# Sliding-window attention and a gated MLP in one kernel: scores of two chunks back to back, and another order for the prologue

## The chip, the cores and the metric

The kernel runs on one core of a Trainium2 chip. The metric is the device time of one execution in microseconds, given as the median of nine executions. The profile comes from one further execution of the same kernel.

## The reference

Attention over q, k and v of the shape 8 batches x 8 heads x 576 positions x 64, where a query sees itself and the 63 positions before it, and then a gated MLP over the 4608 tokens of width 512, with d_ff = 1536:

```python
scores = scale * np.matmul(q, k.transpose(0, 1, 3, 2))        # scale = 1/8
mask = (rel >= 0) & (rel < 64)                                # rel = query position - key position
attn = softmax(where(mask, scores, -1e9));  x = (attn @ v)    # heads laid side by side: 4608 x 512
g = x @ w_gate
out = (g / (1 + exp(-g)) * (x @ w_val)) @ w_out               # 4608 x 512, float32
```

## The kernel before

The 4608 tokens are cut into 36 chunks of 128 tokens for the attention and into 9 blocks of 512 tokens for the MLP; four chunks make a block. TensorE (PE) does all the multiplying, in bf16:

- `S(n)`: the scores of chunk n, sixteen small matmuls (64 rows x 64 columns), into two PSUM banks. ScalarE takes the exponential of each bank into the tile `pt`, and VectorE multiplies it with the 0/1 mask. With `bias` the mask is put in beforehand by two matmuls with `nmask`, and VectorE's two products fall away.
- `AV(n)`: sixteen matmuls of `pt` with the values, two banks; VectorE divides by the sums (`rc`) and writes `xb`.
- `X(n)`: the transpose of `xb` into `xT`, as a DMA transpose on SyncE's queue ("sp"), or on PE with a copy by ScalarE or VectorE.
- `T(n, x)` / `Tpe(n, x, engine)`: the transpose of a loaded k or q chunk into `kT` or `qT`, by a DMA on SP or on PE with a copy.
- `shift(n, part)`: a copy of half a value chunk into `vb` (by DMA on SP, ScalarE or VectorE).
- `F(c, f0, nf, u0, u1)`: for block c, `nf` slices of 128 hidden units by the chunks u0 to u1: matmuls with Wg, ScalarE's tanh into `sig`, matmuls with Wv, and two VectorE operations into `hT`. A block has 12 slices; a full slice is eight matmuls of 128x512.
- `O(c, u)`: twelve matmuls of `hT` with Wo for one chunk of outputs, ScalarE's copy into `ost`, a DMA to memory.

Loads are DMAs issued by GpSimd (POOL), in one queue: `ld` loads a k, q or v chunk (two DMAs where the chunk crosses a batch), `W` some slices of Wg or Wv, `load_wo` half of Wo. A `ld` with a third number also waits until that chunk's scores have run on PE. k and q have rings of four buffers, so a load into a buffer waits until the chunk before it there has been transposed.

Each engine works through its own instructions in the order in which the program lists them, and waits on semaphores. Up to the first instructions of block 2, the order is written out in `PLAN`, a list made beforehand: it starts with clearing tiles (`init_va`, `init_pt` and others), warm-up matmuls on PE (`warm`), the loads, and goes through blocks 0 and 1 of `F`, the outputs of block 0, and the scores up to chunk 12. From block 2 on a loop repeats one period for each chunk.

PSUM has eight banks: four ("f", 0 to 3) for F in turn, one ("o", bank 4) for O, and three ("a", 5 to 7) in turn for scores, AV and transposes. During PLAN, before the first O, bank 4 is in the turn of "a".

Of the kernel before, what the change touches and what calls it, by code (L numbers as in the profile page):

```python
# [5 lines left out]
ALU = mybir.AluOpType  # L6

B, H, S, D = 8, 8, 576, 64
DM, DFF = H * D, 1536
T = B * S  # L10
NCH = T // 128
NFC = T // 512
# [136 lines left out]

class _Kernel:  # L150
    PLAN = [
        ('first_loads', 0), ('init',), ('init_va', 8, 9), ('ld', 'v', 2), ('first_loads', 1), ('init_va', 0, 1),
        ('init_mask',), ('first_cast', 0, 'q', 'act'), ('warm', 4), ('first_cast', 1, 'k', 'act'), ('warm', 5),
        ('ld', 'k', 2), ('init_va', 1, 2), ('first_cast', 1, 'q', 'act'), ('init_va', 6, 7),
        ('first_cast', 0, 'k', 'dve'), ('Tpe', 0, 'k', 'dve'), ('ld', 'q', 2), ('Tpe', 0, 'q', 'dve'), ('warm', 4),
        ('init_pt', 2, 'dve'), ('ld', 'k', 3), ('init_va', 3, 4), ('warm', 2), ('init_kT',), ('init_pt', 1, 'dve'),
        ('shift', 0, 0, 'dve'), ('Tpe', 1, 'k', 'dve'), ('init_va', 2, 3), ('ld', 'v', 1), ('init_pt', 0, 'act'),
        ('ld', 'q', 3), ('shift', 2, 0, 'dve'), ('init_vb',), ('ld', 'k', 4), ('Tpe', 1, 'q', 'act'),
        ('shift', 0, 1, 'act'), ('S', 0, True), ('ld', 'q', 4), ('ld', 'v', 3), ('S', 1, True), ('init_va', 9, 10),
        ('shift', 2, 1, 'dve'), ('ld', 'k', 5), ('Tpe', 2, 'k', 'dve'), ('Tpe', 2, 'q', 'dve'), ('ld', 'q', 5),  # L160
        ('W', 'g', 0, 2), ('init_pt', 3, 'dve'), ('warm', 2), ('Tpe', 3, 'k', 'dve'), ('W', 'v', 0, 2),
        ('ld', 'v', 4), ('shift', 1, 0, 'act'), ('AV', 0), ('S', 2, True), ('init_va', 4, 5), ('init_va', 5, 6),
        ('W', 'g', 2, 4), ('Tpe', 3, 'q', 'dve'), ('shift', 1, 1, 'act'), ('W', 'v', 2, 4), ('AV', 1),
        ('Tpe', 4, 'k', 'dve'), ('W', 'g', 4, 7), ('X', 0, 'act'), ('shift', 3, 0, 'act'), ('Tpe', 4, 'q', 'dve'),
        ('S', 3, True), ('AV', 2), ('S', 4, True), ('W', 'v', 4, 7), ('AV', 3), ('ld', 'q', 7), ('X', 2, 'dve'),
        ('X', 1, 'act'), ('Tpe', 5, 'q', 'dve'), ('ld', 'v', 5), ('Tpe', 5, 'k', 'act'), ('X', 3, 'dve'),
        ('shift', 3, 1, 'act'), ('F', 0, 0, 2, 0, 2), ('W', 'g', 7, 10), ('shift', 4, 0, 'act'), ('ld', 'q', 6),
        ('F', 0, 0, 2, 2, 4), ('AV', 4), ('F', 0, 2, 1, 0, 4), ('S', 5), ('F', 0, 3, 1, 0, 4), ('ld', 'k', 7),
        ('X', 4, 'dve'), ('F', 0, 5, 2, 0, 2), ('F', 0, 4, 3, 3, 4), ('shift', 5, 0, 'act'), ('shift', 5, 1, 'act'),
        ('F', 1, 0, 4, 0, 1), ('W', 'v', 7, 10), ('shift', 4, 1, 'act'), ('Tpe', 7, 'q', 'act'), ('ld', 'k', 6),  # L170
        ('F', 0, 4, 1, 0, 2), ('AV', 5), ('ld', 'k', 9), ('F', 1, 4, 2, 0, 1), ('Tpe', 7, 'k', 'act'),
        ('ld', 'v', 6), ('W', 'g', 10, 12), ('ld', 'q', 9), ('init_va', 7, 8), ('ld', 'k', 8), ('F', 0, 7, 1, 0, 4),
        ('X', 5, 'act'), ('Tpe', 6, 'k', 'dve'), ('Tpe', 6, 'q', 'act'), ('ld', 'k', 10), ('shift', 6, 0, 'act'),
        ('F', 0, 8, 1, 0, 4), ('S', 7), ('F', 1, 0, 4, 1, 2), ('F', 0, 4, 3, 2, 3), ('S', 6), ('ld', 'v', 7),
        ('ld', 'q', 10), ('Tpe', 8, 'k', 'act'), ('F', 0, 9, 1, 0, 4), ('F', 1, 4, 4, 1, 2), ('shift', 6, 1, 'act'),
        ('W', 'v', 10, 12), ('T', 10, 'q'), ('T', 9, 'q'), ('shift', 7, 0, 'act'), ('Tpe', 10, 'k', 'act'),
        ('ld', 'v', 8), ('AV', 6), ('ld', 'q', 8), ('Tpe', 9, 'k', 'act'), ('load_wo', 6, 12), ('F', 0, 10, 1, 0, 4),
        ('load_wo', 0, 6), ('ld', 'k', 11), ('AV', 7), ('X', 6, 'act'), ('F', 0, 11, 1, 0, 4), ('ld', 'q', 11),
        ('ld', 'v', 9), ('Tpe', 8, 'q', 'dve'), ('ld', 'v', 13, 7), ('ld', 'v', 10), ('F', 1, 1, 3, 2, 3),
        ('ld', 'q', 13, 7), ('ld', 'v', 11), ('F', 1, 6, 3, 0, 1), ('shift', 8, 0, 'act'), ('X', 7, 'sp'), ('S', 8),  # L180
        ('S', 10), ('ld', 'v', 12, 6), ('F', 1, 9, 2, 0, 2), ('T', 11, 'q'), ('shift', 7, 1, 'act'), ('S', 9),
        ('O', 0, 0), ('shift', 13, 1, 'sp'), ('F', 1, 0, 1, 2, 4), ('shift', 9, 1, 'act'), ('AV', 8),
        ('ld', 'k', 12, 6), ('ld', 'q', 12, 8), ('shift', 10, 0, 'dve'), ('F', 1, 8, 1, 2, 4),
        ('shift', 11, 1, 'dve'), ('Tpe', 11, 'k', 'act'), ('ld', 'k', 13, 8), ('O', 0, 1), ('ld', 'v', 14, 10),
        ('AV', 10), ('shift', 12, 0, 'sp'), ('shift', 11, 0, 'act'), ('F', 1, 8, 1, 1, 2), ('F', 1, 1, 3, 3, 4),
        ('shift', 9, 0, 'act'), ('T', 12, 'k'), ('shift', 8, 1, 'dve'), ('shift', 10, 1, 'act'), ('S', 11),
        ('O', 0, 2), ('AV', 9), ('T', 12, 'q'), ('X', 8, 'sp'), ('F', 1, 11, 1, 0, 4), ('X', 10, 'sp'), ('AV', 11),
        ('X', 9, 'sp'), ('ld', 'q', 16, 10), ('O', 0, 3), ('T', 13, 'k'), ('F', 1, 4, 4, 2, 3), ('S', 12),
        ('ld', 'k', 14, 10), ('X', 11, 'sp'), ('ld', 'q', 15, 11), ('ld', 'q', 14, 8), ('ld', 'k', 16, 10),
        ('shift', 13, 0, 'sp'), ('shift', 14, 0, 'sp'), ('T', 13, 'q'), ('shift', 12, 1, 'sp'), ('ld', 'v', 16, 10),  # L190
        ('ld', 'k', 15, 11), ('shift', 14, 1, 'sp'), ('ld', 'v', 15, 11), ('ld', 'q', 17, 12), ('ld', 'v', 17, 11),
        ('T', 14, 'k'), ('F', 1, 4, 4, 3, 4), ('T', 14, 'q'), ('F', 1, 9, 2, 2, 4), ('ld', 'k', 17, 12),
    ]

    NQ = 4
# [66 lines left out]
    def segs(self, t0, size):  # L262
        r = 0
        while r < size:
            b, s = divmod(t0 + r, S)
            L = min(size - r, S - s)
            yield r, b, s, L
            r += L
# [123 lines left out]
        b1 = (2 * n + 1) % BPB == 0  # L392
        return slice(2, 4) if b0 else (slice(1, 3) if b1 else slice(0, 2))

    def S(self, n, bias=False):
        if n >= NCH:
            return
        g = self.g
        ip, iz = n % self.NP, n % self.NZ
        pt = self.pt[ip]  # L400
        bx = [self.bank("a"), self.bank("a")]
        sv = [b[0][:, :].rearrange("p (w c q) -> p w c q", w=2, c=4) for b in bx]
        nm = self.nmask[:, :].rearrange("p (a q) -> p a q", a=4)[:, self.var(n)]
        nm = nm.unsqueeze(2).to_broadcast([128, 2, 4, 64])
# [18 lines left out]
        m = self.mask[:, :].rearrange("p (a q) -> p a q", a=4)[:, self.var(n)]  # L423
        m = m.unsqueeze(2).to_broadcast([128, 2, 4, 64])
# [174 lines left out]
    def step(self, op, *a):  # L599
# [16 lines left out]
        else:  # L616
            getattr(self, op)(*a)

    def build(self):
        self.phase = 0  # L620
        self.banks("a", [0, 1, 2, 3, 5, 6, 7])
        for s in self.PLAN:
            self.step(*s)
        for c in range(2, NFC):
            for u in range(4):
                n = 4 * c + u + 4
                self.F(c, 3 * u)
                self.AV(n)
                self.T(n + 3, "k")
                self.X(n)  # L630
                self.T(n + 3, "q")
                self.shift_v(n + 3)
                self.F(c, 3 * u + 1)
                self.S(n + 1)
                self.load(n + 6, after=n + 1)
                late = c == NFC - 1 and u == 3
                if not late:
                    self.O(c - 1, u)
                self.F(c, 3 * u + 2)
                if late:  # L640
                    self.O(c - 1, u)
        self.banks("o", [0, 1, 2, 3])
        for u in range(3):
            self.O(NFC - 1, u)
        self.O_last(NFC - 1, 3)
        self.g.emit()
# [42 lines left out]
```

## Time and profile before

| | us |
|---|---|
| median of nine executions (lowest, highest) | 343.31 (342.4, 348.0) |
| the profiled execution, its time | 344.18 |
| the profiled execution, span from first to last instruction | 342.4 |
| first F on PE | 19.66 |
| first instruction of the loop, F(2, 0), on PE | 88.96 |
| end of the loop, start of the last four outputs, on PE | 329.0 |

The span is counted from the first instruction; times below that have no other unit are us from there. The page's rows give each engine's busy time, then the span in 40 slices with busy tenths, then the DMA queues, the chain of waits that ended last, and groups of instructions with their mean duration. The timeline and the answers by stretch come from the same execution's trace.

### The profile page before, as it was taken

The page shows a single profiled execution, that of the slowest core. Times are in us where ns is not written, and L with a number is a line of the kernel's source. Part 1 is how long each engine was busy: PE and PEld are TensorE (multiplying, and loading weights), DVE is VectorE, ACT ScalarE, POOL GpSimd, SP SyncE. Part 2 cuts the span into 40 slices and gives each one's busy share as a digit, 9 for nine tenths or more (in the row PEclk, how much of TensorE's full clock was granted, in tenths as well). Part 3 has the DMA queues.
Part 4 walks back from the last instruction along what each step waited for, and adds up shares of the span by engine and source line. Part 5 has one row for each costly group of instructions (what it writes and reads, how often), then busy time and mean ns, then how long its engine had stood idle before and what let it go on. Part 6 is the DMA issues. An engine that isn't in the chain of part 4 may idle for free.

```text
span 342.4 us, 7138 instructions
## 1 busy us (share of the span) xinstructions
PE 331.4 (97%) x2879; PEld 177.4 (52%) x2879; DVE 218.2 (64%) x475; ACT 147.8 (43%) x257; POOL 106.9 (31%) x133
## 2 busy tenths in 40 slices
PE   7999998899899999999999999999999999999996
PEld 3568776467444444444444444444444444444444
DVE  5868889276766666666666666666666666655520
ACT  4866777364233444433333444444444443223221
POOL 8994480808053334333333334333300000000000
PEclk9999999899999999999999999999999999999999
DMA  9999999999999999999999999999984411100012
GB/s 161 157 194 183 138 151 163 137 206 127 170 149 220 142 139 146 139 142 137 147 121 161 120 161 144 119 139 142 139 139 103 73 46 48 46 31 34 31 61 95
DMA packets 172001, 43.65 MB, mean 128 GB/s; under 512 B 157568, under 2 KB 167488, under 8 KB 171968
## 3 DMA queue, kind: packets, MB, share of 16 engines
q0 software_dynamic: 115200, 18.36, 77.5%
q1 hardware_dynamic: 49504, 15.00, 29.0%
q10 hardware_dynamic: 7264, 9.83, 8.6%
q8 instruction: 23, 0.38, 0.5%
q14 instruction: 10, 0.08, 0.1%
HBM read 37.75 MB, written 9.44 MB: 138 GB/s over the span
## 4 chain that ended last, share of the span: by engine, by line
PE 90%; POOL 4%; DMA 2%; ACT 2%; DVE 1%; issue 0%; POOLq 0%
PE ps L525 53%; PE ps L564 28%; PE ps L415 3%; PE ps L446 2%; PE ps L445 2%; DMA Wv<-in_moe_w_val_dram 2%; POOL kn L340 1%; POOL qn L340 1%; POOL va L340 1%; ACT pt L428 1%; PE ps L586 1%; ACT sig L541 1%; PE ps L498 1%; ACT vb L272 0%; DVE uu L546 0%; DVE hT L548 0%
## 5 line engine op out<-in xcount | busy, mean ns | idle before, releaser
L546 DVE SCALAR_TENSOR_TENSOR uu<-sig,ps 128x512 bf16<-128x512 bf16 (+3 forms) x112 | 74.4, 665 | 96.4 <-ACT sig L541 95.6
L525 PE MATMUL ps<-xT,Wg 128*128 128x512 bf16 (+2 forms) x572 | 111.9, 327 | 1.6 <-DVE hT L548 1.4
L525 PE MATMUL ps<-xT,Wv 128*128 128x512 bf16 (+2 forms) x572 | 111.9, 327 | 0.3 <-DMA Wv<-in_moe_w_val_dram 0.3
L541 ACT ACTIVATE sig<-ps 128x512 bf16<-128x512 f32 (+3 forms) x112 | 65.1, 582 | 97.7 <-PE ps L525 97.7
L564 PE MATMUL ps<-Wo,hT 128*128 128x512 bf16 x420 | 97.8, 384 | 1.4 <-ACT pt L428 1.4
L548 DVE SCALAR_TENSOR_TENSOR hT<-uu,ps 128x512 bf16<-128x512 bf16 (+3 forms) x112 | 74.8, 668 | 4.0
L525 PEld LDWEIGHTS ps<-xT,Wv 128*128 128x128 bf16 x572 | 50.0, 98 | 44.6 <-issue 0.6
L525 PEld LDWEIGHTS ps<-xT,Wg 128*128 128x128 bf16 x572 | 47.7, 98 | 39.1 <-DVE hT L548 1.6
L340 POOL DMA_DIRECT2D kn<-in_k_dram x38 | 33.1, 882 | 106.0 <-PE ps L415 96.5
L564 PEld LDWEIGHTS ps<-Wo,hT 128*128 128x128 bf16 x420 | 39.4, 99 | 47.1 <-issue 2.2
L569 ACT ACTIVATE ost<-ps 128x512 f32<-128x512 f32 x35 | 20.9, 597 | 67.7 <-PE ps L564 67.7
L428 ACT ACTIVATE pt<-ps 128x512 bf16<-128x512 f32 x72 | 38.7, 594 | 17.0 <-PE ps L415 16.9
L340 POOL DMA_DIRECT2D qn<-in_q_dram x38 | 33.2, 880 | 30.9 <-DMA qT<-qn 30.9
L340 POOL DMA_DIRECT2D va<-in_v_dram x40 | 35.2, 897 | 0.8 <-DVE wz L277 0.8
L455 DVE TENSOR_TENSOR xb<-ps,rc 128x256 bf16<-128x256 f32 x72 | 30.5, 424 | 2.5
L430 DVE TENSOR_TENSOR pt<-pt,mask 128x512 bf16<-128x512 bf16 x62 | 23.9, 419 | 1.4 <-ACT pt L428 0.9
L446 PE MATMUL ps<-va,pt 128*128 128x65 bf16 x288 | 22.5, 194 | 0.0
L445 PE MATMUL ps<-vb,pt 128*128 128x65 bf16 x288 | 22.4, 193 | 0.1
L445 PEld LDWEIGHTS ps<-vb,pt 128*128 128x128 bf16 x288 | 20.1, 98 | 3.7 <-ACT pt L428 0.2
L446 PEld LDWEIGHTS ps<-va,pt 128*128 128x128 bf16 x288 | 18.9, 97 | 3.3
L415 PEld LDWEIGHTS ps<-qT,kT 64*128 64x128 bf16 x576 | 10.4, 95 | 15.4 <-DVE rc L452 9.3
L415 PE MATMUL ps<-qT,kT 64*128 64x64 bf16 x576 | 14.5, 191 | 2.0 <-ACT vb L272 1.6
(48 smaller groups left out, 97.1 us busy)
## 6 DMA issues: line engine op xcount, KB each, us to landing
out_dram<-ost ACTq DMA_DIRECT2D x35, 256.0 KB, 4.4
va<-in_v_dram POOLq DMA_DIRECT2D x32, 128.0 KB, 6.7
kn<-in_k_dram POOLq DMA_DIRECT2D x30, 128.0 KB, 4.8
qn<-in_q_dram POOLq DMA_DIRECT2D x30, 128.0 KB, 5.9
vb<-va SPq DMA_DIRECT2D x47, 80.0 KB, 5.1
Wo<-in_moe_w_out_dram POOLq DMA_DIRECT2D x2, 768.0 KB, 14.6
Wg<-in_moe_w_gate_dram POOLq DMA_DIRECT2D x3, 256.0 KB, 7.6
Wv<-in_moe_w_val_dram POOLq DMA_DIRECT2D x3, 256.0 KB, 7.0
```

The costliest lines, as they stand in the source:

```text
L340: self.g.op("pool", lambda e, d=d, a=a: e.dma_start(d, a), reads=gate, writes=ks, dma=True)
L415: r = e.matmul(sv[p][:, w, c], self.kT[ps, c, k0:k0 + 128], self.qT[ps, c, self.qs(n, 64 * w, 64 * w + 64)], start=not bias, stop=not bias ...
L428: g.op("act", lambda e, po=po, p=p: e.activation(po, sv[p], ACTF.Exp, scale=SCALE), reads=[bx[p][1]], writes=[pk])
L430: g.op("dve", lambda e, po=po: e.tensor_tensor(po, po, m, ALU.mult), reads=[pk, "mask"], writes=[pk])
L445: e.matmul(av[:, j, :], pt[:, h, 0:128], vb[:, h, 0:65], start=True, stop=False)
L446: r = e.matmul(av[:, j, :], pt[:, h, 64:192], va[:, h, 0:65], start=False, stop=True)
L455: g.op("dve", lambda e, xo=xo, av=av, rb=rb: e.tensor_tensor(xo, av[:, :, 0:64], rb, ALU.mult), reads=[bk, ("rc", ir)], writes=[("xb", ix, ...
L525: r = e.matmul(bank[:, w * j:w * j + w], W[:, kk, f * 128:f * 128 + 128], xT[:, kk, 128 * u0:128 * u1], start=(kk == 0), stop=(kk == NK - 1))
L541: g.op("act", lambda e: e.activation(sig[:, 0:n], G[:, 0:n], ACTF.Tanh, scale=0.5), reads=[gk], writes=[("sig", i)])
L546: g.op("dve", lambda e: e.scalar_tensor_tensor(uu[:, 0:n], sig[:, 0:n], 1.0, G[:, 0:n], ALU.add, ALU.mult), reads=[("sig", i), gk], writes ...
L548: g.op("dve", lambda e: e.scalar_tensor_tensor(d, r3(uu[:, 0:n]), 0.5, r3(V[:, 0:n]), ALU.mult, ALU.mult), reads=[("uu", i), vk], writes=[ ...
L564: r = e.matmul(OB[:, :], hT[:, f, 128 * u:128 * u + 128], self.Wo[:, f, :], start=(f == 0), stop=(f == NF - 1))
```

## The change

The loop goes by two chunks at a time. In each such period, the scores of two chunks stand next to each other on PE, one further chunk ahead than before, and so do the transposes of k and q (four chunks ahead of n instead of three). One of the two banks that the first of the two chunks needs is bank 4, the bank of the outputs. The two outputs of a period stand at its end with one F between them. The PLAN is a new list: it uses the same steps in another order, with other engines for many copies, some other chunks (scores up to chunk 13, transposes up to chunk 15 in part), 15 instead of 17 warm-up matmuls, and six chunks with `bias` instead of five.

```diff
-    def S(self, n, bias=False):
+    def S(self, n, bias=False, o=False):
...
-        bx = [self.bank("a"), self.bank("a")]
+        bx = [self.bank("o" if o else "a"), self.bank("a")]
...
+    def period(self, c, u):
+        n = 4 * c + u + 4
+        sh = lambda m: [("shift_v", m)]
+        p = [("F", c, 3 * u), ("AV", n), ("T", n + 4, "k"), ("X", n), ("T", n + 4, "q")] + sh(n + 4)
+        p += [("F", c, 3 * u + 1), ("AV", n + 1), ("T", n + 5, "k"), ("X", n + 1), ("T", n + 5, "q")] + sh(n + 5)
+        p += [("F", c, 3 * u + 2), ("F", c, 3 * u + 3), ("S", n + 2, False, True), ("S", n + 3)]
+        p += [("ld", "kqv", n + 6, n + 2), ("ld", "kqv", n + 7, n + 3), ("F", c, 3 * u + 4), ("O", c - 1, u)]
+        tail = [("F", c, 3 * u + 5), ("O", c - 1, u + 1)]
+        return p + tail
...
         for c in range(2, NFC):
-            for u in range(4):
-                n = 4 * c + u + 4
-                self.F(c, 3 * u)
-                self.AV(n)
-                self.T(n + 3, "k")
-                self.X(n)
-                self.T(n + 3, "q")
-                self.shift_v(n + 3)
-                self.F(c, 3 * u + 1)
-                self.S(n + 1)
-                self.load(n + 6, after=n + 1)
...
-                    self.O(c - 1, u)
-                self.F(c, 3 * u + 2)
...
+            for u in (0, 2):
+                for s in self.period(c, u):
+                    self.step(*s)
```

Of the new PLAN, the parts that the prediction speaks of (the list has 226 steps):

```diff
+        ('first_loads', 0), ('init_va', 3, 4), ('init_va', 0, 1), ('first_loads', 1), ('init_va', 5, 6),
+        ('init_va', 1, 2), ('init_va', 2, 3), ('init_va', 7, 8), ('init',), ('init_pt', 1, 'act'),
+        ('first_cast', 0, 'k', 'act'), ('init_kT',), ('init_pt', 3, 'act'), ('ld', 'k', 5), ('ld', 'q', 4),
+        ('init_va', 8, 9), ('warm', 7), ('init_pt', 2, 'act'), ('ld', 'k', 2), ('init_mask',),
...
+        ('Tpe', 7, 'k', 'act'), ('Tpe', 6, 'q', 'dve'), ('Tpe', 7, 'q', 'dve'), ('W', 'g', 3, 4), ('X', 3, 'act'),
+        ('W', 'g', 4, 6), ('shift', 4, 0, 'dve'), ('W', 'v', 4, 6), ('W', 'g', 10, 12), ('ld', 'v', 5),
+        ('shift', 3, 1, 'act'), ('X', 2, 'dve'), ('Tpe', 5, 'q', 'dve'), ('S', 6, False, False), ('W', 'v', 10, 12),
+        ('S', 7, True, False), ('AV', 4), ('W', 'g', 0, 3), ('W', 'v', 0, 3), ('F', 0, 3, 1, 0, 4), ('ld', 'q', 8),
...
+        ('S', 10, False, False), ('ld', 'v', 11), ('S', 8, False, False), ('F', 1, 0, 2, 2, 4),
...
+        ('shift', 9, 1, 'act'), ('S', 11, False, False), ('F', 1, 10, 2, 1, 3), ('O', 0, 3), ('shift', 10, 0, 'act'),
...
+        ('AV', 10), ('F', 1, 3, 2, 1, 3), ('ld', 'q', 14, 9), ('S', 13, False, False), ('S', 12, False, True),
+        ('X', 9, 'sp'), ('F', 1, 2, 1, 0, 4), ('F', 1, 3, 1, 3, 4), ('ld', 'k', 16, 12), ('ld', 'k', 14, 8),
+        ('shift', 12, 0, 'sp'), ('ld', 'v', 14, 10), ('ld', 'k', 17, 11), ('X', 11, 'sp'), ('X', 10, 'sp'),
+        ('T', 15, 'q'), ('T', 14, 'q'), ('T', 14, 'k'), ('ld', 'q', 16, 11), ('ld', 'v', 15, 9), ('ld', 'q', 17, 11),
```

## The prediction

> **What bounds the kernel now.** The page first: PE is busy for 97% of the span, and from slice 15 on it has no gap.
>
> ```profile
> PE 331.4 (97%) x2879; PEld 177.4 (52%) x2879; DVE 218.2 (64%) x475; ACT 147.8 (43%) x257; POOL 106.9 (31%) x133
> PE   7999998899899999999999999999999999999996
> DVE  5868889276766666666666666666666666655520
> PEclk9999999899999999999999999999999999999999
> DMA  9999999999999999999999999999984411100012
> ```
>
> So a gain must come from less time per PE instruction, or from the gaps of the first 90 us. The slice with PEclk 8 (60 to 68 us) lies where PE stood still. The answer by stretches shows how costly that was:
>
> ```profile
> 58.30:61.75 3.45, 0.41 (x16) 0.35 (x17) 2.70 (x6) 2.58 (x5) 1.64 (x3) 1.00 2.40 118
> 61.75:66.20 4.45, 4.45 (x14) 1.77 (x15) 0.18 (x1) 0.00 (x0) 4.45 (x6) 0.62 2.41 153
> ```
>
> PE worked 0.41 us in 3.45; then the first output's twelve matmuls took 4.44 us at a clock of 0.62 instead of 2.59. The chain of waits blames ScalarE, but the landing times of single DMAs, asked by tile, fit better: the transpose of q9, issued at 46.26, landed 13.6 us later at 59.86, and S(9) starts at 59.95; the second half of Wo, issued at 44.65, landed after 17.1 us at 61.75, and O starts at 61.75. Likewise X(11), issued at 81.10, landed at 88.9 (7.8 us), and the loop starts at 88.96. The prologue's late waits are waits for DMAs.
>
> ```profile
> 44.75 3.47 SPq L387 DMA_TRANSPOSE qT<-qn  x2
> 43.80 1.70 POOL L373 DMA_DIRECT2D Wo<-in_moe_w_out_dram  x2
> 81.10 1.22 SPq L467 DMA_TRANSPOSE xT<-xb  x1
> ```
>
> The timeline of PE gives the price of scores: one chunk in the loop, then chunks 8 and 10 in the prologue, which stand together already.
>
> ```profile
> 205.58 1.03 PE L525 MATMUL ps<-xT,Wv 128*128 128x512 bf16 x4
> 206.54 0.41 PE L415 MATMUL ps<-qT,kT 64*128 64x64 bf16 x16
> 206.88 2.76 PE L564 MATMUL ps<-Wo,hT 128*128 128x512 bf16 x12
> ```
>
> ```profile
> 55.04 0.83 PE L525 MATMUL ps<-xT,Wv 128*128 128x128 bf16 x12
> 55.80 0.64 PE L415 MATMUL ps<-qT,kT 64*128 64x64 bf16 x32
> 56.38 0.39 PE L525 MATMUL ps<-xT,Wg 128*128 128x256 bf16 x2
> ```
>
> Ends are modelled, so I count from start to start: 512 columns take 0.216 us, four of them end at 206.44, and O starts at 206.88: 0.44 us for one chunk. In the second case twelve of 128 columns end at 55.71 and F starts at 56.38: 0.67 for two.
>
> **The loop.** A pair saves 2 x 0.44 - 0.67 = 0.21 us. Eleven pairs stand in the loop: 2.3. The new PLAN has done S(13) as well, so one score fewer is left: 0.44. The 0.32 us that S(13) waits at 93.38 belongs to a transpose of q13 (issued 84.15, 9.1 us) and goes too. All else in the loop is the same work.
>
> Does the new order make a wait? Times from the period's start, with a full F at 1.73, AV 0.49, O 2.59. Bank use goes seven steps per period through three banks. The tightest: the second half of AV(n+1) needs the bank of AV(n)'s first half. In the trace VectorE frees that 3.65 us after the start of the F before (202.50 to 206.15); PE asks at 1.73 + 0.49 + 1.73 + 0.24 = 4.19. Four F stand between VectorE's backlog (two AV, 1.2 each) and the scores: its product for the last F ends at 9.4, that of the one whose bank is needed at 7.9, while PE asks at 8.6. Bank 4 is free for O at 9.0, when the first exponential is done, and PE asks at 10.3. On ScalarE four exponentials of 0.54 hold back the next tanh to 10.6; O covers it, with F's next need of a bank at 12.9. On SP, X(n+1) goes out at about 9.3 behind three transposes and two shifts; block c+1 asks at 17.3, so 8 us stay where calm landings take 2.4 to 5. The six loads go out in one bunch after S(n+3), but their readers come a period later. I cost these edits at zero; without the cover, 0.5 us in each of twelve periods would be 6 us.
>
> **The prologue until the first F.** Before, F starts at 19.66. After, weights come later in POOL's queue. An issue there takes 0.87 us (0.67 for a half chunk), the first Wg was issued at 13.13 behind 9 whole and 2 split chunks and landed 6.4 later. Now 13 whole and 3 split chunks stand ahead: 2.6 + 13 x 0.87 + 3 x 1.35 + 0.75 (Wv) = 18.8, some 0.2 for waits on ring buffers (k7 waits for Tpe of k3, q7 for that of q3 at about 14.2), 6.2 to land: 25.2. PE's own chain to there (q1 landed 7.55, k5 8.8, q4 9.9, scores from 11.4, v4 landed 24.1, AV(4)) fits before it. So the two more bias matmuls (0.43), one Tpe and one X more (0.22 each) and two warm-ups fewer cost nothing: PE waits for weights there. They would cost 0.87 if it did not.
>
> Two things may move this start. The six memsets now ahead of wz (0.15 each, 0.9 together) run while POOL writes its first DMAs. In the trace, two of them beside the first value load stretched its issue from 0.90 to 1.01: by that row about 0.2 in all, which the 25.2 has room for. [...] Second, PE has little to do from 6.8 to 10.3 (about 1.1 us in 3.4). [...] The rows above say that 0.41 us of work in 3.45 is not enough, so the limit isn't complete idleness; whether 1.1 is enough no row shows. If not, scores and AV from 11.4 take 1.5 longer, and through q3 and q2 the loads also. I take zero, and keep 1.5.
>
> **From the first F to the loop.** Work that is left on PE, by counting the list: F 24 x 1.728 = 41.5, O 4 x 2.59 = 10.4, seven scores 3.1, seven AV 3.4, ten transposes of 0.22: 60.5 (before: 61.9, in 69.3 us, so 7.4 were lost). Three pairs save 0.6. Losses now: weights. Between 19.5 and 41.1 twenty slices and ten chunks landed: 0.86 a chunk, 0.65 a slice. By this Wv[5] lands 0.2 after it is asked for and later ones just in time: 0.3. Small gaps as before (1.2 in the 38 us to 58): 1.0. Then, 32 chunks stand ahead of Wo where 27 stood, 5 x 0.86: Wo lands at 66.0, asked for at 65.2. And S(8) needs kT8 at about 58.5: k8 lands at 49.5, T(8) goes out behind T(11), and takes 6 as in calm times or 11.1 to 13.6 as beside Wo, so 56 to 63. The two waits overlap: I take 1.5, with ends 0 and 4.5. The loop starts at 25.2 + 60.5 - 0.6 + 0.3 + 1.0 + 1.5 = 87.9, 1.1 earlier.
>
> **A new wait at the join.** POOL's load of k16 waits for S(12), and behind it are k14, v14, k17 and five others. S(12) runs 5.4 us before the loop; k14 is issued some 4.2 before it, lands after 6.6 (second in the like bunch at 78), and then T(14) takes 6 to 9 us. S(14) is asked for 8.0 into the loop: late by 0.4 to 3.4. I take 1.5.
>
> Sum against the profiled execution: -1.1 - 2.3 - 0.4 - 0.3 + 1.5 = -2.6, span 339.8, time 341.6. That execution lay 0.9 above the median of the nine, so on the median: 340.7.
>
> **The rivals.**
>
> Fewer late waits. The DMA engines are quieter when T(8) and T(14) come, and both waits vanish: 3.0 less, 337.7. For it: in the loop a transpose lands after 4.4 to 7.1. Against: the DMA row is at 9 all through the prologue.
>
> Transposes starved beside Wo (slower). T(8) is the place. If it takes the 13.6 us of q9, S(8) starts at 63.2, 4.7 late; the clock then falls as it did at 61.75 (4.44 for 2.59, 1.85). That is 3.2 + 1.85 more than I took: 345.7. It decides from a landing at about 61.5 on. For it: both transposes beside Wo took over 11 us. Against: T(8) leaves a little earlier against Wo's data, and only one transpose is ahead of it in its queue. [...]
>
> No net effect. The pairs save less, as the 0.67 is one row of the prologue, or each period meets a short wait: 0.2 us a period more gives the 2.3 back, 343.
>
> **How the numbers follow.** 0.3%, or 1.0 us, is about what a measurement of this kernel can tell from no change. The forecast 340.7 has 0.46, the fewer waits 0.14: faster 0.60. No net effect 0.13. Starved transposes, and what pushes with them, 0.27. The range from 337.0 to 346.0 takes in the ends of the two unknown waits (-3.0, +4.9 with the clock) and leaves two in ten out. The forecast's own range is 338.5 to 342.3.
>
> **What would show it.** Right: 0.67 us between the F ahead of two scores and the F behind, in all eleven pairs; periods of two chunks at 17.2 us where two took 17.4; first F on PE near 25; the loop starting near 88; a PE gap ahead of S(14) of 1 to 2 us. Wrong: a wait ahead of AV(n+1) or F in every period; the clock row under 9 near 10 or near 60 us; S(8) behind T(8) after 61.5; block starts of the loop that wait for X.

## The result: 0.8% faster, with one late transpose left in

| | before | after |
|---|---|---|
| median, us (lowest, highest) | 343.66 (339.68, 348.0), 54 runs | 340.71 (337.59, 343.32), 17 runs |
| ratio of after to before, 95% interval | | 0.9922 [0.9897, 0.9947] |
| profiled execution: time, span | 344.18, 342.4 | 344.31, 342.3 |
| first F on PE | 19.66 | 23.88 |
| first F to F(2, 0), the loop's first instruction | 69.30 | 67.93 |
| F(2, 0) to the end of the span | 253.4 | 250.5 |

The profiled execution of after lies above all of its timed runs, so its span alone would say "no change"; it is read here for where time goes, and the medians for how much. Ratios, here and below, are taken over those executions that lie within 1.5% of the fastest of their kernel, and so are not just the quotient of the medians. The page of after, the same rows as those shown of before:

```profile
PE 329.6 (96%) x2903; PEld 180.8 (53%) x2903; DVE 220.9 (65%) x477; ACT 145.3 (42%) x258; POOL 108.4 (32%) x135
PE   5999999699999999999999999999999999999996
DVE  3787878486793939393939394949484848383610
PEclk9999999899999999999999999999999999999999
DMA  9999999997999999999896989798973202001022
```

PE is still the bound. Its row has a hole in slice 8 (60 to 68 us), and the clock row falls there again, as before. VectorE's row now swings between 3 and 9: its work comes in bunches of two chunks, and PE's row beside it does not dip.

The loop's price is in PE's timeline (start, duration, engine, line, operation):

```profile
126.19 1.03 PE L530 MATMUL ps<-xT,Wg 128*128 128x512 bf16 x4
133.21 1.03 PE L530 MATMUL ps<-xT,Wv 128*128 128x512 bf16 x4
134.17 0.64 PE L420 MATMUL ps<-qT,kT 64*128 64x64 bf16 x32
134.74 1.04 PE L530 MATMUL ps<-xT,Wg 128*128 128x512 bf16 x4
143.39 1.03 PE L530 MATMUL ps<-xT,Wg 128*128 128x512 bf16 x4
```

Thirty-two score matmuls stand in one row. The F ahead of them ends at 133.21 + 4 x 0.216 = 134.07, the next starts at 134.74: 0.67 us for two chunks. One period goes from 126.19 to 143.39: 17.20. Both are the forecast's figures.

The hole in slice 8, in PE's waits and in its timeline (in brackets: idle before, and what ended it):

```profile
PE ps L420 <- DMA kT<-kn: 3.5, 1, 3.5
```

```profile
58.65 0.41 PE L420 MATMUL ps<-qT,kT 64*128 64x64 bf16 x16
62.52 0.41 PE L420 MATMUL ps<-qT,kT 64*128 64x64 bf16 x16 [3.47 <-DMA kT<-kn]
62.87 1.40 PE L530 MATMUL ps<-xT,Wg 128*128 128x256 bf16 x8
64.06 1.91 PE L530 MATMUL ps<-xT,Wv 128*128 128x256 bf16 x8
65.77 1.57 PE L530 MATMUL ps<-xT,Wg 128*128 128x128 bf16 x16
70.49 2.75 PE L569 MATMUL ps<-Wo,hT 128*128 128x512 bf16 x12
```

S(10) is done at 59; S(8) waits for `T(8, 'k')` until 62.52. The F pieces behind it then take 1.40, 1.91 and 1.57 where 1.04 to 1.06 is full rate. By single DMAs: k8's transpose was issued at 49.8 and landed 12.6 us later. What the clock did, by stretch (length, then PE, PEld, DVE, ACT, POOL busy, granted clock, DMA share, GB/s):

```profile
58.99:62.46 3.47, 0.07 (x6) 0.00 (x0) 1.62 (x4) 1.09 (x2) 0.00 (x0) 1.00 1.41 186
62.46:66.70 4.24, 4.18 (x41) 3.37 (x42) 2.16 (x4) 2.42 (x4) 2.64 (x3) 0.61 1.65 114
```

So this execution shows the rival "transposes starved beside Wo" as to the wait and the clock. The question for the experiments is how much of the median this costs, what else the prologue and the loop each bring, and what the shared bank is for.

### The profile page after: what moved, and what is told of

Its sections match the earlier page's. It is cut to its first block, busy times and chain, and to the rows that moved or that the text cites. A ratio compares the mean times of both kernels' runs of the same rounds, so it can differ in the third digit from the quotient of the medians.

```text
span 342.3 us, 7184 instructions
## 1 busy us (share of the span) xinstructions
PE 329.6 (96%) x2903; PEld 180.8 (53%) x2903; DVE 220.9 (65%) x477; ACT 145.3 (42%) x258; POOL 108.4 (32%) x135
## 4 chain that ended last, share of the span: by engine, by line
PE 82%; DMA 9%; POOL 6%; issue 1%; ACT 0%; ACTq 0%; DVE 0%
PE ps L530 47%; PE ps L569 26%; DMA kn<-in_k_dram 4%; DMA kT<-kn 4%; PE ps L420 2%; PE ps L451 2%; PE ps L450 2%; DMA hT<-in_q_dram 2%; POOL qn L345 2%; POOL Wg L373 1%; POOL va L345 1%; POOL kn L345 1%; POOL Wv L373 1%; PE ps L591 1%; PE ps L503 1%
## 5 line engine op out<-in xcount | busy, mean ns | idle before, releaser
L530 PE MATMUL ps<-xT,Wg 128*128 128x512 bf16 (+2 forms) x580 | 113.1, 327 | 0.9 <-DMA Wg<-in_moe_w_gate_dram 0.8
L569 PE MATMUL ps<-Wo,hT 128*128 128x512 bf16 x420 | 95.9, 379 | 0.0
L530 PEld LDWEIGHTS ps<-xT,Wv 128*128 128x128 bf16 x580 | 51.5, 98 | 44.7 <-DVE hT L553 0.8
L530 PEld LDWEIGHTS ps<-xT,Wg 128*128 128x128 bf16 x580 | 48.4, 99 | 36.7 <-issue 1.0
L569 PEld LDWEIGHTS ps<-Wo,hT 128*128 128x128 bf16 x420 | 41.0, 98 | 48.6
L433 ACT ACTIVATE pt<-ps 128x512 bf16<-128x512 f32 x72 | 37.5, 599 | 11.7 <-PE ps L420 11.6
L345 POOL DMA_DIRECT2D va<-in_v_dram x40 | 36.5, 933 | 0.8 <-POOLq L675 0.8
L420 PEld LDWEIGHTS ps<-qT,kT 64*128 64x128 bf16 x576 | 9.7, 95 | 11.8 <-issue 11.4
L420 PE MATMUL ps<-qT,kT 64*128 64x64 bf16 x576 | 12.4, 191 | 3.5 <-DMA kT<-kn 3.5
```

Source lines behind the costliest of these rows:

```text
L345: self.g.op("pool", lambda e, d=d, a=a: e.dma_start(d, a), reads=gate, writes=ks, dma=True)
L420: r = e.matmul(sv[p][:, w, c], self.kT[ps, c, k0:k0 + 128], self.qT[ps, c, self.qs(n, 64 * w, 64 * w + 64)], start=not bias, stop=not bias ...
L433: g.op("act", lambda e, po=po, p=p: e.activation(po, sv[p], ACTF.Exp, scale=SCALE), reads=[bx[p][1]], writes=[pk])
L530: r = e.matmul(bank[:, w * j:w * j + w], W[:, kk, f * 128:f * 128 + 128], xT[:, kk, 128 * u0:128 * u1], start=(kk == 0), stop=(kk == NK - 1))
L569: r = e.matmul(OB[:, :], hT[:, f, 128 * u:128 * u + 128], self.Wo[:, f, :], start=(f == 0), stop=(f == NF - 1))
```

## The experiments

All were run with the kernel before on the same chip. Its median was 343.96 us in the first four, 342.7 in the next four, 342.97 in the last two, so ratios are what is compared.

**1 and 2. Each half of the change alone.** The old PLAN with the new loop (the first two chunks of block 2 in old periods, then one extra score, so that the pairs can start; ten pairs):

```diff
+        for u in range(2):
...
+        self.S(15)
+        self.T(17, "k")
+        self.T(17, "q")
+        self.shift_v(17)
         for c in range(2, NFC):
-            for u in (0, 2):
+            for u in ((2,) if c == 2 else (0, 2)):
```

> The old PLAN and the first two periods of the old loop, then the new two-chunk periods from chunk 14 on (S(15) and the transposes of chunk 17 are put in once to join them). Ten pairs of scores. Theory (a pair saves 0.21 us of PE time and nothing else in the loop changes): 2.1 us less than before, about 341.4 against 343.5, ratio 0.994; two chunks go by in 17.20 us instead of 17.40. Rival (the loop gives nothing, all of the gain is the prologue's): ratio 1.000. Rival (the new period has waits of its own that the new PLAN hides): over 1.000.

Measured: 341.75 us, ratio 0.9953 [0.9916, 0.9990]. In its profile two chunks go by in 17.20 us, and F(2, 0) to the end takes 251.3 us, 2.1 less than before: what ten pairs were expected to save.

The new PLAN with the loop of before (its first transposes and score left out, as PLAN has done them):

```diff
-            for u in (0, 2):
-                for s in self.period(c, u):
-                    self.step(*s)
+            for u in range(4):
+                first = c == 2 and u == 0
...
+                if not first:
+                    self.S(n + 1)
```

> The new PLAN with the old one-chunk loop (its first period leaves out S(13) and the transposes of chunk 15, which the new PLAN has done). Theory (the loop is worth 2.3 us, the prologue's order itself nearly nothing, 0.5 to 1): about 343.0, ratio 0.997 to 1.000. Rival (the new prologue carries the gain): ratio 0.993 as with both parts.

Measured: 341.25 us, ratio 0.9935 [0.9898, 0.9972]. This is better than the theory, which had put most of the gain into the loop. Its profile (span 339.6) says why: k8's transpose landed after 10.2 us, S(8) waited 0.84, and the clock stayed up:

```profile
58.02 0.41 PE L420 MATMUL ps<-qT,kT 64*128 64x64 bf16 x16 [0.84 <-DMA kT<-kn]
58.36 1.05 PE L530 MATMUL ps<-xT,Wg 128*128 128x256 bf16 x8
```

F(2, 0) starts at 85.64 there, 3.3 before the old kernel's 88.96, and the rest takes 253.96 us, about what it took before (253.4). So both halves bring something: the loop some 3 us (250.5 to 253.4 in the profiles of after and before; the pairs, one score fewer and the wait of S(13) together), the prologue up to 3.3 if its transpose is in time. The intervals of both runs overlap, and neither alone is told apart from the whole change; the split rests on the profiles.

**3. The late transpose taken out of the DMA queue.** k8 goes through PE (0.22 us and a copy by ScalarE):

```diff
-        ('T', 8, 'k'), ('F', 0, 6, 3, 0, 1),
+        ('Tpe', 8, 'k', 'act'), ('F', 0, 6, 3, 0, 1),
```

> The changed kernel with one step other: the transpose of k8 goes through PE and a ScalarE copy instead of a DMA on SP. Theory (S(8) waits up to 3.5 us for that DMA, which lands between the two halves of Wo, and the clock then runs at half for some 4 us): no gap ahead of S(8), no fall of the clock, O(0,3) then waits only for Wo at about 65.5 instead of 70.5; span near 337.5, time near 339, ratio to before 0.985 to 0.988, that is 1.5 to 2.5 below the changed kernel's median. Rival (Wo or the transposes of chunks 12 and 13 are late next and take the gain): ratio 0.992 as the changed kernel. Rival (the wait is only in the one profiled execution): 0.992 too, but without a gap elsewhere.

Measured: 339.86 us, ratio 0.9874 [0.9831, 0.9917], span 336.5. S(8) and S(10) stand in one row, F runs at full rate behind them, and the clock stays up; F(2, 0) starts at 85.70 instead of 91.81. And what is late next comes into sight, at the join of PLAN and loop:

```profile
57.84 0.64 PE L420 MATMUL ps<-qT,kT 64*128 64x64 bf16 x32
94.40 0.64 PE L420 MATMUL ps<-qT,kT 64*128 64x64 bf16 x32 [0.66 <-DMA kT<-kn]
```

S(14) waits 0.66 us for its transpose. In the profile of after it did not wait. That is not because the loop came 6 us later there: the load of k14 stands behind a wait for S(12) on PE and came 6 us later too. The load and the transpose landed sooner, after 4.3 and 6.5 us, where they took 4.7 and 7.9 here.

**4. The pairs taken apart.** One F between the two chunks of a loop period:

```diff
-        p += [("F", c, 3 * u + 2), ("F", c, 3 * u + 3), ("S", n + 2, False, True), ("S", n + 3)]
+        p += [("F", c, 3 * u + 2), ("S", n + 2, False, True), ("F", c, 3 * u + 3), ("S", n + 3)]
```

> The changed kernel with the two scores of a period apart: the first stands ahead of the fourth F, the second behind it; all else is as changed. Theory (the loop's gain is that two scores stand together, 0.21 us each time): eleven pairs lost, 2.3 us slower than the changed kernel, about 343.0, ratio to before 0.999. Rival (the gain is in the later transposes and loads or in the shared bank, not in the neighbourhood on PE): ratio 0.992, as the changed kernel.

Measured: 346.28 us, ratio 1.0057 [1.0021, 1.0092], slower than expected. PE's timeline gives the pair its price: from one S(n+2) at 131.46 to the next at 148.87 it is 17.41 us instead of 17.20, so eleven periods lose 2.3. The rest of the difference to after is elsewhere: the first of the two chunks is now asked for one F earlier, and S(14) waits at the join.

```profile
131.46 0.41 PE L420 MATMUL ps<-qT,kT 64*128 64x64 bf16 x16
148.87 0.41 PE L420 MATMUL ps<-qT,kT 64*128 64x64 bf16 x16
96.64 0.41 PE L420 MATMUL ps<-qT,kT 64*128 64x64 bf16 x16 [1.68 <-DVE hT L553]
59.37 0.41 PE L420 MATMUL ps<-qT,kT 64*128 64x64 bf16 x16 [2.08 <-DMA kT<-kn]
60.74 1.91 PE L530 MATMUL ps<-xT,Wv 128*128 128x256 bf16 x8
```

The first two rows are S(n+2) of two periods, the third is S(14), the last two are S(8) and the F behind it. The row of S(14) names VectorE, but by single DMAs the transpose of k14, issued at 89.31, landed 7.2 us later at 96.5, and S(14) starts at 96.64. So the gain of the pair is 0.2 us a period, and the period's order also gives the transposes one F more of slack, which matters at the join. From F(2, 0) to the end the split kernel took 254.6 us against 250.5: 2.3 + 1.7, and 0.1 that I have not placed. The ratios differ by more, 0.0135 or 4.6 us; a part of that can be the clock, which fell in more executions of this run (see T(8) below).

**5. S(8) later in the program.** The two F pieces that stand behind S(8) go ahead of it:

```diff
-        ('S', 10, False, False), ('ld', 'v', 11), ('S', 8, False, False), ('F', 1, 0, 2, 2, 4),
+        ('S', 10, False, False), ('ld', 'v', 11), ('F', 1, 0, 2, 2, 4), ('F', 1, 8, 4, 3, 4), ('S', 8, False, False),
```

> In the changed kernel S(8) stood idle 3.47 us for the transpose of k8, and the two F pieces behind it, 1.04 + 1.04 each by their rows at full rate, waited with it and then ran at half clock for a further 2 us or so. Here those two pieces (3.5 us of matmuls) stand ahead of S(8), in program order only. Theory (the loss of the changed kernel at this place is one wait and the clock that it costs; nothing behind needs S(8) before AV(8) after the O tile): S(8) waits under 1 us, the clock stays at full rate from 60 to 70 us, 2 to 5 us gone in runs where the transpose is late: ratio to the kernel before 0.985 to 0.989. Rival (AV(8) is close behind S(8) in need, so the wait moves on to it by way of exp and mask): AV(8) waits 1 us or more, ratio 0.990 to 0.993. Rival (PE does not set the time here): no change from 0.992.

Measured: 338.53 us, ratio 0.9914 [0.9884, 0.9945], span 335.8. k8's transpose was no faster (11.8 us); PE had work while it came, the clock stayed at 1.00, and AV(8) did not wait. In place of 3.47 us stands a wait of 0.95, of S(11) for a bank that an exponential still reads, since three scores now follow one another with the two of S(8) and S(9):

```profile
62.37 0.41 PE L420 MATMUL ps<-qT,kT 64*128 64x64 bf16 x16 [0.95 <-ACT pt L433]
```

The ratio falls short of what was expected, though the profile is as the theory said; the interval reaches into the expected range.

**6. The wait kept, the clock held.** Eight matmuls of 128x512 on zeros between S(10) and S(8):

```diff
-        ('S', 10, False, False), ('ld', 'v', 11), ('S', 8, False, False),
+        ('S', 10, False, False), ('ld', 'v', 11), ('warm', 8), ('S', 8, False, False),
```

> Eight matmuls of 128x512 on zeros, 1.7 us at full rate and without use, stand between S(10) and S(8); the transpose of k8 and all else are left as they are. It parts the wait from the clock. Theory (the late transpose costs twice: the wait itself, then about 2 us of matmuls at half clock): in a run with a late transpose S(8) still starts at its landing, but the F rows behind it stay at 1.04 us and the clock of 60 to 70 us at 1.00; in a run with a wait under 1.7 us the filling costs up to 1.7 less that wait; median ratio 0.988 to 0.992. Rival (the half clock would have come anyway, or costs nothing because what follows waits for Wo): ratio 0.993 to 0.996, that is the changed kernel plus the filling.

Measured: 341.54 us, ratio 0.9968 [0.9940, 0.9997]: by the figures nearest to the rival, just above its range. The profile doesn't support the rival's reason, though. The transpose was late as in after (12.7 us), S(8) waited 1.14 behind the filling, and F behind it ran at 1.05 with the clock at 1.00, as the theory said. But the filling costs 1.7 us (8 x 0.216) in every run, and a run gets its price back only if the transpose is late enough and the clock would have fallen. And S(14) waited 1.56. So this did not settle what the clock costs on the median; the next comparison does better.

What the fall costs is seen by laying two profiles side by side. In run 9 below (PLAN unchanged up to here) S(8) also came late, but the clock did not fall. From S(8) to O it took 59.88 to 66.20, 6.32 us; in after 62.52 to 70.49, 7.97: the fall costs 1.65 us.

**7. Half of Wo later.**

```diff
-        ('load_wo', 0, 6), ('X', 6, 'act'), ('Tpe', 10, 'q', 'act'), ('load_wo', 6, 12), ('ld', 'v', 10),
+        ('load_wo', 0, 6), ('X', 6, 'act'), ('Tpe', 10, 'q', 'act'), ('ld', 'v', 10),
...
-        ('S', 10, False, False), ('ld', 'v', 11), ('S', 8, False, False),
+        ('S', 10, False, False), ('ld', 'v', 11), ('load_wo', 6, 12), ('S', 8, False, False),
```

> The second half of Wo (768 KB) is issued behind the loads of v10, q13, k12 and v11 on POOL, some 10 us later, so that half as much of Wo moves beside the transposes of k11 and k8. Theory (those transposes land late, after 11.0 and 12.6 us, because they share the DMA engines with Wo): the transpose of k8 lands in 6 to 9 us, S(8) waits under 0.5 us, full clock from 60 to 70 us; the O tile may now wait for Wo up to 3 us, 0 if the half lands in 14 us or less; ratio 0.986 to 0.990. Rival (it is not Wo but the order on SP, or the loads of v and q, that delays the transpose): it still lands after 10 us or more and S(8) waits as before, ratio 0.992 or, with a wait of O on top, 0.994 to 1.000.

Measured: 347.38 us, ratio 1.0164 [1.0127, 1.0200]. My expectation of the issue time was wrong. Ahead of the half stands the load of k12, which overwrites the buffer of k8 and so waits on POOL until k8 has been transposed:

```profile
58.78 0.89 POOL L345 DMA_DIRECT2D kn<-in_k_dram  x1 [7.05 <-DMA kT<-kn]
60.52 0.84 POOL L378 DMA_DIRECT2D Wo<-in_moe_w_out_dram  x1
```

The half was issued 19 us later than in after, not 10, and O waited for it:

```profile
71.37 3.90 PE L569 MATMUL ps<-Wo,hT 128*128 128x512 bf16 x11 [6.47 <-issue]
```

The accident bears on the other question. No byte of the second half was under way while k8 was being transposed, and the transpose took 10.2 us all the same, as in run 2, where all of Wo was beside it; S(8) waited 1.17. So it is late without the second half of Wo. A small share of that half is not ruled out: the eight profiles with this transpose have 10.2 to 12.7. Nor was the other rival tried, the order on SP: the transpose of k11 stands ahead of that of k8, and in all eight k8 landed 4.5 to 5.8 us behind it.

**8. k8 on PE, and k14's load ahead of k16's.** Run 3 with the join mended: k16's load waits for S(12), and k14's stood behind it in POOL's queue.

```diff
-        ('F', 1, 3, 1, 3, 4), ('ld', 'k', 16, 12), ('ld', 'k', 14, 8),
+        ('F', 1, 3, 1, 3, 4), ('ld', 'k', 14, 8), ('ld', 'k', 16, 12),
```

> The changed kernel with the transpose of k8 on PE (339.86 us, 0.9874, where S(14) waited 0.66 us at the start of the loop for its transpose of k14) and the load of k14 ahead of that of k16 on POOL, where it stood behind a wait of 13.8 us. Theory (the wait of S(14) at the join is the load of k14 issued late, and comes into sight once S(8) is no longer late): no wait of S(14), 0.5 to 1 us gone: ratio 0.983 to 0.987, span about 335.8. Rival (the wait comes from the transposes in SP's order, not from the load): S(14) still waits 0.5 us or more, ratio 0.987 to 0.989.

Measured: 338.01 us (337.72 to 338.54), ratio 0.9883 [0.9853, 0.9914], span 336.2. POOL's timeline, first of run 3, then of this run:

```profile
80.86 1.75 POOL L345 DMA_DIRECT2D kn<-in_k_dram  x2 [13.72 <-PE ps L420]
```

```profile
67.27 0.91 POOL L345 DMA_DIRECT2D kn<-in_k_dram  x1
81.01 0.88 POOL L345 DMA_DIRECT2D kn<-in_k_dram  x1 [12.83 <-PE ps L420]
```

k14 now goes out at 67.27 instead of 81.7, its transpose at 83.25 instead of 86.48, and S(14) does not wait. The gain of this over run 3, 0.66 by the profile, is less than the ratios can tell. What stands out is the spread: 0.8 us from lowest to highest, where after has 5.7.

**9. No shared bank.** The first chunk of a loop pair takes two of the three "a" banks:

```diff
-        p += [("F", c, 3 * u + 2), ("F", c, 3 * u + 3), ("S", n + 2, False, True), ("S", n + 3)]
+        p += [("F", c, 3 * u + 2), ("F", c, 3 * u + 3), ("S", n + 2), ("S", n + 3)]
```

> The changed kernel, but S(n+2) of a loop pair takes two of the three score banks instead of one of them and the bank of the output tile; the prologue keeps its own. S(n+3) then needs as its second bank the first one of S(n+2), which is free when the exp of 0.52 us has read it. Theory (the shared bank is what makes the pair possible: without it S(n+3) waits for that exp): 0.8 us of wait and the 0.2 us saved by the pair, about 1.0 a period, are lost in 10 periods: 349 to 351 us, ratio 1.013 to 1.020. Rival (the bank of the output tile is itself in use until the O tile's result is copied, so that sharing it costs about as much as it saves): ratio 0.990 to 0.996.

Measured: 349.06 us, ratio 1.0207 [1.0146, 1.0267]. Each pair is broken by a wait for the exponential of its own first half:

```profile
131.96 0.41 PE L420 MATMUL ps<-qT,kT 64*128 64x64 bf16 x16
133.06 0.41 PE L420 MATMUL ps<-qT,kT 64*128 64x64 bf16 x16 [0.69 <-ACT pt L433]
150.03 0.41 PE L420 MATMUL ps<-qT,kT 64*128 64x64 bf16 x16
```

Eleven waits, 7.6 us in all; a period takes 18.07 instead of 17.20 (the start of S(n+2) to that of the next, 150.03). Eleven times 0.87 is 9.6 us; the ratios of this kernel and of after differ by 0.0285, or 9.8. So the shared bank is what makes the pair possible: without it the two-chunk period is slower than two old ones (17.4).

**10. Order alone.** Run 5 and k14's load first, with no instruction changed in kind:

> The changed kernel in program order alone: S(8) behind the two F pieces (as in the run where the ratio was 0.9914 with a median of 338.53 us) and the load of k14 ahead of that of k16. No instruction is added or changed. Theory (both late waits of the changed kernel, S(8) and S(14), are matters of order): no wait of S(8) or S(14) over 0.3 us, full clock from 60 to 70 us, 337 to 338.5 us, ratio 0.983 to 0.989. Rival (the early load of k14 competes with Wo and the loads before the loop, so that something else is late): ratio 0.990 to 0.993.

Measured: 338.5 us (337.89 to 339.38), ratio 0.9881 [0.9843, 0.9919], span 337.3. No wait of S(8) or S(14), full clock; S(11)'s 0.95 is left, and this execution also waited 0.9 for Wg at 26.6. Runs 8 and 10 beat the kernel before and aren't told apart from each other; against after their ratios are 0.004 lower, with intervals that just overlap.

## Why the prediction came out as it did

Forecast 340.7, measured 340.71. That is closer than the steps deserve, and in part luck: the profiled execution took 2.5 us more than forecast, and lay 3.6 above the median where I had allowed 0.9. Against the profiled execution, which was forecast at a span of 339.8 and took 342.3:

| step | forecast | profile of after | difference |
|---|---|---|---|
| first F | 25.2 | 23.88 | -1.3 |
| first F to the loop | 62.7 | 67.93 | +5.2 |
| loop to the end, with the join wait | 251.9 | 250.5 | -1.4 |

- **The pair and the loop.** Right in size: 0.67 us, 17.20 a period, and S(13)'s wait and one score gone. No period waits for banks, the backlog of VectorE or X: of waits, PE has none in after from 94 us to the end. Run 9 shows that this was no idle worry: the cover of one bank is worth 0.87 us a period. The rival "no net effect" fell: run 1, the loop alone, saved what its ten pairs were to save.
- **First F.** The count of POOL's issues was good: the first Wg went out at 19.26, forecast 18.8 (the terms add up to 18.7) and 0.2 of waits. It landed in 4.5 us, where I took 6.2. The memsets cost nothing that shows: POOL's first issue took 1.01 us before and after, so the 0.11 that I had put down to two memsets did not grow with more of them. PE's thin stretch at 7 to 10 us (1.21 us of work in 3.0) did not lower the clock, as I took it: it was 1.00 there and in the window behind, 8.80 to 12.22. The window (as counted in the last section) from 5.39 to 8.80 had 1.84 us of work, above the limit found there. The chance of 0.27 also counted in what pushes with starved transposes; no run shows a term for that, and these two readings are what was found in its place.
- **Weights.** A term mis-sized: I gave 0.3; the waits behind the first F are 0.52, 0.31 and 0.66, 1.5 in all. The last is named `hT`, but by single DMAs Wv's slices 8 and 9, issued at 30.24, landed 14.4 us later, at 44.6, and F starts at 44.75:

```profile
26.29 1.02 PE L530 MATMUL ps<-xT,Wg 128*128 128x512 bf16 x4 [0.52 <-DMA Wg<-in_moe_w_gate_dram]
27.62 1.02 PE L530 MATMUL ps<-xT,Wv 128*128 128x512 bf16 x4 [0.31 <-DMA Wv<-in_moe_w_val_dram]
44.75 0.83 PE L530 MATMUL ps<-xT,Wv 128*128 128x128 bf16 x12 [0.66 <-DVE hT L553]
```

- **T(8).** Taken as 1.5 with ends 0 and 4.5. The profile has 3.47 and 1.65 for the clock, 5.1 in all, beyond the end; the rival had this case. With the 1.2 too little for weights, the 3.6 too little here make 4.8 of the 5.2 in the table. It is not every run's case: the wait was 0.84 in run 2, 2.08 in run 4 and 2.67 in run 9, with this part of PLAN the same in all. How often the clock fell can be read from its mean in each timed execution, 0.995 where it ran at half rate once for 3.4 us: in 6 of the 17 of after (median 342.15 us, the other eleven 339.33) and, counting one at 0.99, in 8 of the 12 of run 4. It is on record at 0.999 or 1.00 in all 42 of runs 3, 5, 6, 8 and 10, which leave no long pause ahead of S(8). The ratios fit a mean loss between none and 5.1: 0.9922 for after, 0.9883 and 0.9881 for runs 8 and 10 without the wait, a difference of 0.004 or 1.3 us, with intervals that just overlap, and up to 0.7 of it may be the join's. The rival's reason, Wo, is not shown: in run 7 the transpose was late without the second half. What makes these transposes land after 10 to 13 us is open; the DMA row is at 9 beside them, but so it is in stretches where they land faster.
- **The join.** Forecast 1.5, found 0 in after, 0.34 in run 7, 0.66 in run 3, 1.56 in run 6, 1.68 in run 4. The mechanism was right, and run 8 removed it at the place named (k14's load behind k16's wait). The sizes were not: in after the load went out 4.0 us before the loop (forecast 4.2) but landed after 4.3 (forecast 6.6), the transpose after 6.5. A late S(8) does not give S(14) more time, since k14's load waits for S(12) on PE and is late with it: in run 7, where O had waited 6.47, S(14) still waited.

## What to carry to other kernels

Put two small groups of matmuls of one kind together only after finding them the PSUM banks: the 0.2 us that a pair saves was lost four times over (0.87 a period in run 9) where the second waited for the first's exponential. Behind any late DMA in front of a filled engine, ask first whether other work already in the list can stand ahead of the waiting instruction: order alone took away the wait and the clock's fall (run 5) and, with one load moved as well, most of the spread (run 10, though of six executions only). When summing waits of a list, ask of each late transfer what it waits for itself: a load that waits for work of the late engine is late with it, and an earlier wait hides nothing of the later one (in run 7 O had waited 6.47 us, and S(14) still waited 0.34).

## What the hardware showed that I had not expected

The fall of the clock does not follow the length of the wait. It came after PE had done next to nothing for 3.45 us (before), 3.47 (after), 2.08 (run 4) and 6.47 (run 7). It did not come after 2.67 (run 9), nor in run 1, where S(9) waited 2.83 for its q and the first output another 0.79 behind it. Run 9's F behind the wait, to be laid beside the 1.91 of run 4 after a shorter one:

```profile
59.88 0.41 PE L420 MATMUL ps<-qT,kT 64*128 64x64 bf16 x16 [2.67 <-DMA kT<-kn]
61.11 1.04 PE L530 MATMUL ps<-xT,Wv 128*128 128x256 bf16 x8
```

The clock records show one length again and again. The half rate lasted 3.41 us in before, after and run 4, and twice that, 6.83, in run 7. The slow start shows in the warm-up matmuls of 128x512: in before the first nine took 3.54 us, six at 5.77 took 1.46; in after seven took 3.17, six at 5.52 took 1.46. By the clock records of the traces, the fall lies a whole number of 3.413 us behind the rise that ended the slow start: 17 in before (4.21 to 62.23) and after (5.39 to 63.41), 16 in run 4 (5.82 to 60.43), 18 in run 7 (5.86 to 67.30). With windows of 3.413 us counted on from that rise (5.66 in run 1, 7.81 in run 9), these are the two at the pause, in pairs for before, after, run 4, run 1 and run 9 (columns as in the stretches above, the clock third from the end):

```profile
58.82:62.23 3.41, 0.89 (x19) 0.59 (x20) 2.43 (x5) 2.06 (x4) 2.12 (x3) 1.00 2.57 111
62.23:65.65 3.42, 3.42 (x10) 1.23 (x9) 0.00 (x0) 0.00 (x0) 3.42 (x6) 0.50 2.41 153
60.00:63.41 3.41, 0.89 (x21) 0.82 (x22) 0.64 (x2) 0.62 (x2) 0.72 (x1) 1.00 1.63 182
63.41:66.83 3.42, 3.42 (x23) 2.68 (x22) 2.26 (x5) 1.98 (x4) 1.92 (x3) 0.50 1.53 103
57.01:60.43 3.42, 1.34 (x39) 1.13 (x35) 1.82 (x4) 1.70 (x4) 0.90 (x2) 1.00 1.25 205
60.43:63.84 3.41, 3.41 (x25) 2.79 (x24) 2.54 (x5) 1.80 (x3) 1.74 (x2) 0.50 2.13 165
56.86:60.27 3.41, 1.48 (x14) 1.08 (x12) 2.94 (x6) 2.53 (x5) 0.00 (x0) 1.00 1.48 167
60.27:63.69 3.42, 1.72 (x23) 0.95 (x24) 0.85 (x2) 1.09 (x2) 2.35 (x4) 1.00 2.91 117
55.59:59.01 3.42, 1.62 (x28) 1.19 (x26) 2.51 (x6) 1.89 (x4) 0.00 (x0) 1.00 1.41 143
59.01:62.42 3.41, 2.54 (x40) 2.33 (x41) 1.33 (x3) 2.06 (x4) 2.38 (x3) 1.00 1.34 200
```

Where PE had worked 0.89 or 1.34 us of a window, the next ran at half rate; where it had worked 1.48 or 1.62, it did not. So it is in all windows of the ten profiles that have a clock record: each with at most 1.34 us was followed by half rate, none with 1.48 or more. By these profiles, then, the same pause costs the clock or not by where the windows lie in it, and they lie differently in each execution (the rise came at 4.21 to 7.81 us in the six named). No run varied that on purpose; the limit is read from these profiles alone.

The clock explains only a part of the spread. After's runs differ by 5.7 us, but its eleven at full clock still by 4.1, and so do run 5's twelve, which all kept the clock. It was smallest where k14's load was moved too: 0.8 in run 8 and 1.5 in run 10, against 2.7 in run 3, which has k8 on PE alone, of six executions each.

A transpose by DMA of one chunk (128 KB) issued between 44 and 50 us landed after 8.4 to 15.1 us in the twelve profiles, one issued between 69 and 110 us after 2.3 to 9.4; the DMA engines were busy in both stretches (DMA share 1.77 and 1.49 in after), and no single neighbour was found that explains the former.
